# GpSimd's subtractions issued in pieces of at most 256 columns, in a kernel of one transform and two networks

## The chip, the core and the metric

The kernel runs on one core of a Trainium2 chip. A core has five engines that run their own instruction streams and wait for one another by semaphores: TensorE (PE in the profile, its weight loads PEld), VectorE (DVE), ScalarE (ACT), GpSimd (POOL) and SyncE (SP), which here issues the DMAs. The metric is the device time of one execution in microseconds; less is better.

## The reference

```python
def _attn_ref(x):                      # x: (2, 3008, 256)
    X = np.fft.fft(x, axis=1)
    X = np.fft.fft(X, axis=2)
    return X.real.astype(np.float32)

def _moe_ref(x, w_in, w_out):          # 6016 tokens, 256 -> 2048 -> 256
    h = x @ w_in
    r = np.maximum(h, 0.0)
    g = r * r
    return (g @ w_out).astype(np.float32)

def _moe2_ref(x, w_in, w_out):         # the same sizes
    h = x @ w_in
    g = h * (1.0 / (1.0 + np.exp(-1.702 * h)))
    return (g @ w_out).astype(np.float32)
```

The real part of a two-dimensional Fourier transform feeds a first network with a squared ReLU, whose output feeds a second network with a sigmoid gate. All of it is in single precision (the weights arrive as float64 and are narrowed on the chip).

## The kernel before

**Numbers as two parts.** The kernel's matmuls take operands of type `fp32r`, to which a cast loses bits of the float32. So each operand `x` is kept as a high part, a cast of `x` by ScalarE, and a low part `x - high`, a subtraction. A product is three matmuls: high x high, high x low and low x high. The low parts are all made by one helper:

```python
def sub(eng, o, a, b):
    eng.tensor_tensor(out=o, in0=a, in1=f32(b), op=ALU.subtract)
```

`eng` is VectorE (`V`) or GpSimd (`G`). As the helper is one line, every such subtraction has line L75 in the profile, on either engine; they are told apart by the tile that they write.

**Who calls it.** `low_part` (L700) makes `gl`, the low part of a hidden activation: two rows of 376 or 378 columns, on GpSimd in 113 of 128 steps and on VectorE in the steps of `VSTEPS`. `split_eo` (L335) makes the low part of `eo`, the transformed input. `widen` (L175) does it for a weight tile `w` of 1024 columns, on the engine that the table `LOW` names. `widen_in` (L209) prepares the second network's first weights: four sums on GpSimd (L221), then for each of two rows a pair of subtractions into `w2i`, of 512 columns (four groups of 128) and 384 columns (three groups of 128). `split` and the second network's `gl` (L830) use VectorE alone.

**First stage (to about 528 us).** A loop of 128 steps works through the first network. The tokens are 8 blocks (2 batches x 4 groups of frequencies) of 376 or 378 columns times two rows; a step is one block and one of 16 groups of 128 hidden features. In a step:

- `front1` issues six matmuls (L429 to L431) into one of two `psa` buffers in PSUM
- VectorE makes `p` (L686) and the two halves of `h` (L688, L689) out of that buffer, which frees it
- ScalarE takes the ReLU (L695) and the square (L696), and casts the high part `gh` (L698); in the steps of `SV` VectorE does ReLU and square in one (L693)
- `low_part` of the step before is issued: `gl = h - gh`. Tiles of `h` have four buffers, those of `gh` and `gl` five each
- `back` issues the 12 matmuls (L444) of the step four earlier (`LAG`), from its `gh` and `gl`
- `background(i)` adds items of other work, by the table `PLAN` (first step, items a step, last step). From step 18 on, background work of VectorE and ScalarE is queued behind the step's own.

Background work is the folds and the transform of the inputs (L260 to L278, L293, L332), and the preparation of weights: `narrow` turns the two 32-bit words of a float64 into a float32 in about six operations of 1024 columns (L157 to L168, most on VectorE), then `widen` or `widen_in` casts and subtracts. Near the end, the first block of the second network's input is added up and differenced on GpSimd (L581, L591).

In this stage the order of instructions on each engine is set by a planner: it takes ready instructions by priority (their order in the code) on times that it models, so an engine's order can differ from the code's.

**Second stage (from about 528 us).** The second network, 64 units of two hidden groups in a seven-product scheme (L737) with its second matmuls (L753), is written in the order of issue by hand (`manual_schedule`). Its low parts are VectorE's; GpSimd has only L581 and L591.

Of the kernel before, what the change touches and what calls it, by code (L numbers as in the profile page):

```python
# [13 lines left out]
ALU = mybir.AluOpType  # L14
# [48 lines left out]
def spectral_two_mlps_kernel(  # L63
# [5 lines left out]
    V, A, G, T = nc.vector, nc.scalar, nc.gpsimd, nc.tensor  # L69

    def f32(ap):
        return ap.bitcast(F32)

    def sub(eng, o, a, b):
        eng.tensor_tensor(out=o, in0=a, in1=f32(b), op=ALU.subtract)  # L75


    psa = ctx.enter_context(tc.tile_pool(name="psa", bufs=2, space=PSUM))
# [96 lines left out]
    def widen(mlp, kind, g, temps, dest, then=None, tag="xt"):  # L175
        low = G if LOW[mlp, kind, g] == "G" else V
        raw = raws.pop((mlp, kind, g))
        ue = temp(temps, tag)
        yield from narrow(raw, ue, (mlp, kind, g))
        if then:  # L180
            then()
        w = dest.tile([P, 2, 1024], F32R, tag="w", name="w")
        o = ue[:, 0]
        if (mlp, kind) == (0, 0):

            o = ue[:, 1]
            a, c = ue[:, 0, 0:512], ue[:, 0, 512:1024]
            yield lambda: (G if g in EOG else V).tensor_tensor(out=o[:, 0:512], in0=a, in1=c, op=ALU.add)
            yield lambda: V.scalar_tensor_tensor(out=o[:, 512:1024], in0=a, scalar=mask, in1=c,
                                                 op0=ALU.mult, op1=ALU.subtract)  # L190
        yield lambda: A.copy(w[:, 0], o)
        yield lambda: sub(low, w[:, 1], o, w[:, 0])
        if mlp and (kind, g) in PARKED:
            park((mlp, kind, g), w)
        weights[mlp, kind, g] = w
# [13 lines left out]
    def widen_in(g, ue, dest, then=None):  # L209

        raw = raws.pop((1, 0, g))
        yield from narrow(raw, ue, (1, 0, g))
        if then:
            then()
        a = ue[:, 0].rearrange("p (k r f c) -> p k r f c", k=2, r=2, f=2)
        t = ue[:, 1].rearrange("p (i r c) -> p i r c", i=4, r=2)
        a11, a21, a12, a22 = (a[:, k, :, f] for k in range(2) for f in range(2))
        s2, s3, s4 = (t[:, i] for i in range(3))
        for o, x, y, op in ((s3, a11, a21, ALU.subtract), (a21, a21, a22, ALU.add), (s2, a21, a11, ALU.subtract),
                            (s4, a12, s2, ALU.subtract)):  # L220
            yield lambda: G.tensor_tensor(out=o, in0=x, in1=y, op=op)  # L221
        for r in range(2):
            w = dest.tile([P, 2, 1024], F32R, tag="w", name="w2i")
            parts = []
            for lo, hi, x in ((0, 4, a[:, :, r]), (4, 7, t[:, 0:3, r])):
                o = w[:, :, lo * P:hi * P]
                o = o.rearrange("p h (k f c) -> p h k f c", k=2, f=2) if lo == 0 else o.rearrange("p h (i c) -> p h i c", c=P)
                parts.append((o[:, 0], o[:, 1], x))
            yield lambda: [A.copy(o, x) for o, _, x in parts]
            yield lambda: [sub(G, l, x, o) for o, l, x in parts]  # L230
            if (0, g) in PARKED:
                park((1, 0, 2 * g + r), w)
            weights[1, 0, 2 * g + r] = w
# [101 lines left out]
    def split_eo(b, kb, e):  # L335
        wd = WID[kb]
        low = V if LOWE[b, kb] == "V" else G
        t = ep.tile([P, 2, 2, NP], F32R, tag="eo", name="eo")
        for r in (slice(0, 1), slice(1, 2)) if (b, kb) in FINE else (slice(0, 2),):
            A.copy(t[:, r, 0, 0:wd], e[:, r, 0:wd])  # L340
            sub(low, t[:, r, 1, 0:wd], e[:, r, 0:wd], t[:, r, 0, 0:wd])
        eo[b, kb] = t
# [317 lines left out]
    for i in range(n):  # L660
# [19 lines left out]
        elif done:  # L680
# [6 lines left out]
                               in1=ps[:, 0, 0:wd], op0=ALU.mult, op1=ALU.add)  # L687
# [74 lines left out]
    with tc.manual_schedule():  # L762
        for u in range(units + 2):
# [41 lines left out]
            if here:  # L805
                if p == 7 and j < BLKS - 1:
                    run(stage_a(j + 1))
                if rest is not None and not run(rest, 3 if j else (0, 2, 2, 4, 4, 4, 4, 4)[p]):
# [8 lines left out]
                                in1=cd[:, :, 0:wd], op=ALU.add)  # L817
# [20 lines left out]
        o = m3.tile([P, 2, NP], F32, tag="o", name="o")  # L838
# [133 lines left out]
```

## Time and profile before

| what | us |
|---|---|
| median of 3 runs | 1037.11 (1035.15 to 1038.47) |
| profiled execution, its own time | 1035.54 |
| span of its instructions | 1033.8 |
| TensorE busy | 971.6 |
| VectorE busy | 817.1 |
| ScalarE busy | 616.4 |
| GpSimd busy | 351.4, in 216 instructions |

The profile is one execution. The span runs from the first instruction to the last; the rest of the execution's time lies around it. Busy times are sums over the whole span, and the two stages differ: the share of an engine in one of them is read from a view by stretch. A duration of VectorE or GpSimd runs from the start of an instruction to its end, with whatever held it up once it had started; a wait for another engine's result lies ahead of the start and is shown as idle time with the releaser.

### The profile page before, as it was taken

To read this page: it belongs to the slowest core of one execution; us is meant where nothing else is said; L and a number is where in the kernel's file an instruction comes from. 1 tells how busy PE (TensorE), PEld (TensorE's weight loads), DVE (VectorE), ACT (ScalarE), POOL (GpSimd) and SP (SyncE) were. 2 spreads that over 40 slices of the span, in tenths; PEclk is the share of its full clock that TensorE was granted. 3 is DMA by queue.
4 is the path that set the end of the run, shared out by engine and by line. 5 is a ranking of instruction groups with operands and counts; after the bars stand their busy time and mean duration, and the time that the engine had idled before them with its cause. 6 is when DMAs were issued, how large, how long until landed. Compare 5 with 4: busy or idle time off the path is not lost.

```text
span 1033.8 us, 14043 instructions
## 1 busy us (share of the span) xinstructions
PE 971.6 (94%) x5496; PEld 939.3 (91%) x5496; DVE 817.1 (79%) x1088; ACT 616.4 (60%) x764; POOL 351.4 (34%) x216
## 2 busy tenths in 40 slices
PE   4879997899989999999989999999999999999998
PEld 4569887899989889898989999999999999999997
DVE  7995889886777579777658888887988888888875
ACT  2667576775788578797754554554555445454443
POOL 2546464444567446786815210102020020200000
PEclk9999999999999999999999999999999999999999
DMA  7531112101132112101342101000100001000000
GB/s 289 204 127 61 71 71 82 71 31 53 42 129 96 72 55 99 71 31 60 120 132 93 60 31 31 30 31 5 57 1 31 30 26 35 1 31 1 30 1 30
DMA packets 22914, 65.22 MB, mean 63 GB/s; under 512 B 1856, under 2 KB 14272, under 8 KB 19648
## 3 DMA queue, kind: packets, MB, share of 16 engines
q1 hardware_dynamic: 22848, 64.32, 17.4%
q8 instruction: 43, 0.70, 0.3%
q14 instruction: 23, 0.19, 0.1%
HBM read 43.13 MB, written 21.19 MB: 62 GB/s over the span
## 4 chain that ended last, share of the span: by engine, by line
PE 47%; DVE 5%; ACT 4%; issue 1%; POOL 1%; DMA 0%; DVEq 0%; POOLq 0%; ACTq 0%
PE psb L753 24%; PE psa L737 22%; ACT h L696 1%; ACT h L695 1%; DVE gl L75 1%; PE psb L444 1%; ACT gh L698 1%; POOL gl L75 1%; DVE g L789 0%; DVE ue L168 0%; DVE h L689 0%; DMA ydram<-o 0%; DVE p L686 0%; POOL raw L581 0%; DVE h L688 0%
## 5 line engine op out<-in xcount | busy, mean ns | idle before, releaser
L75 POOL TENSOR_TENSOR gl<-h,gh 128x752 fp32r<-128x752 f32 (+1 forms) x113 | 216.0, 1920 | 166.6 <-ACT gh L698 142.1
L444 PE MATMUL psb<-gh,w 128*128 128x376 f32 (+1 forms) x1024 | 240.6, 340 | 4.4 <-ACT o L557 3.5
L753 PE MATMUL psb<-gh,w 128*128 128x376 f32 (+1 forms) x1024 | 237.7, 334 | 0.0
L444 PEld LDWEIGHTS psb<-gh,w 128*128 128x128 f32 x1024 | 185.6, 192 | 6.8 <-ACT o L557 4.7
L753 PEld LDWEIGHTS psb<-gh,w 128*128 128x128 f32 x1024 | 182.9, 188 | 0.0
L695 ACT ACTIVATE h<-h 128x752 f32<-128x752 f32 (+1 forms) x116 | 96.5, 833 | 81.7 <-DVE h L689 77.8
L444 PE MATMUL psb<-gl,w 128*128 128x376 f32 (+1 forms) x512 | 133.7, 341 | 3.2 <-POOL gl L75 2.8
L818 ACT ACTIVATE g<-c 128x1128 f32<-128x1128 f32 (+1 forms) x64 | 73.7, 1152 | 100.1 <-DVE c L816 100.1
L753 PE MATMUL psb<-gl,w 128*128 128x376 f32 (+1 forms) x512 | 129.9, 335 | 0.4 <-DVE gl L75 0.3
L686 DVE SCALAR_TENSOR_TENSOR p<-n,w1n_t,psa 128x376 f32<-128x376 f32 (+1 forms) x128 | 76.5, 601 | 59.7 <-PE psa L431 59.5
L698 ACT CAST gh<-h 128x752 fp32r<-128x752 f32 (+1 forms) x128 | 105.0, 822 | 21.5 <-DVE h L693 14.0
L75 DVE TENSOR_TENSOR gl<-g,gh 128x1504 fp32r<-128x1504 f32 (+1 forms) x64 | 112.2, 1753 | 1.6 <-ACT gh L798 1.6
L429 PE MATMUL psa<-eo,w 128*128 128x376 f32 (+1 forms) x256 | 89.9, 351 | 24.6 <-DVE h L689 19.9
L798 ACT CAST gh<-g 128x1504 fp32r<-128x1504 f32 (+1 forms) x64 | 93.1, 1454 | 32.2 <-DVE g L789 32.2
L591 POOL TENSOR_TENSOR ue<-raw 128x376 f32<-128x376 f32 (+1 forms) x16 | 19.6, 1243 | 271.0 <-DVE ya L75 270.8
L444 PEld LDWEIGHTS psb<-gl,w 128*128 128x128 f32 x512 | 94.6, 193 | 4.8 <-POOL gl L75 4.0
L696 ACT ACTIVATE h<-h 128x752 f32<-128x752 f32 (+1 forms) x116 | 96.6, 834 | 3.2
L753 PEld LDWEIGHTS psb<-gl,w 128*128 128x128 f32 x512 | 92.2, 188 | 1.0 <-DVE gl L75 1.0
L789 DVE TENSOR_TENSOR g<-g,c 128x1128 f32<-128x1128 f32 (+1 forms) x64 | 89.6, 1401 | 1.2 <-ACT g L818 1.2
L815 DVE TENSOR_TENSOR g<-g,psa 128x376 f32<-128x376 f32 (+1 forms) x64 | 35.0, 547 | 68.5 <-ACT g L814 68.5
L430 PE MATMUL psa<-eo,w 128*128 128x376 f32 (+1 forms) x256 | 86.4, 338 | 0.7 <-DVE eo L75 0.7
L431 PE MATMUL psa<-eo,w 128*128 128x376 f32 (+1 forms) x256 | 86.2, 337 | 0.0
(135 smaller groups left out, 1594.3 us busy)
## 6 DMA issues: line engine op xcount, KB each, us to landing
ydram<-o SPq DMA_DIRECT2D x18, 376.0 KB, 2.9
xt<-in_x SPq DMA_DIRECT2D x5, 1024.0 KB, 7.1
cst<-in_dfts SPq DMA_DIRECT2D x8, 570.0 KB, 5.5
raw<-ydram SPq DMA_DIRECT2D x6, 752.0 KB, 4.5
out<-o SPq DMA_DIRECT2D x11, 376.0 KB, 3.1
raw<-in_w1i SPq DMA_DIRECT2D x4, 1024.0 KB, 5.6
raw<-in_w1o SPq DMA_DIRECT2D x4, 1024.0 KB, 4.9
raw<-in_w2i SPq DMA_DIRECT2D x4, 1024.0 KB, 4.9
```

Of the source, the lines that this page charges most:

```text
L75: eng.tensor_tensor(out=o, in0=a, in1=f32(b), op=ALU.subtract)
L429: T.matmul(o, lhsT=w[:, 0, fs], rhs=t[:, par, 0, 0:wd], start=True, stop=False)
L430: T.matmul(o, lhsT=w[:, 0, fs], rhs=t[:, par, 1, 0:wd], start=False, stop=False)
L431: T.matmul(o, lhsT=w[:, 1, fs], rhs=t[:, par, 0, 0:wd], start=False, stop=True)
L444: T.matmul(acc[j][ec][:, s, 0:wd], lhsT=w[:, hl, e0:e0 + P], rhs=(gh, gl)[gi][:, s, 0:wd], start=(first and hl == 0 and gi == 0), stop=(la ...
L695: A.activation(out=hv, in_=hv, func=AF.Relu)
L696: A.activation(out=hv, in_=hv, func=AF.Square)
L698: last_a = A.copy(gh[:, :, 0:wd], hv)
L737: T.matmul(bank, lhsT=w[:, hl, slot * P:(slot + 1) * P], rhs=t[:, yl, i], start=(first and hl == 0 and yl == 0), stop=(hl == 1), skip_grou ...
L753: T.matmul(o[:, s, 0:wd], lhsT=w[:, hl, e0:e0 + P], rhs=g[:, 2 * i + s, 0:wd], start=(f == 0 and hl == 0 and g is gh), stop=(f == 15 and h ...
L789: V.tensor_tensor(out=g[:, 1:4, 0:pw], in0=g[:, 1:4, 0:pw], in1=c[:, :, 0:pw], op=ALU.mult)
L798: A.copy(gh[:, :, 0:pw], g[:, :, 0:pw])
```

## The change

The helper splits what it issues to GpSimd. A tile with more than two dimensions is taken apart along its second one until pieces are rows; a row of `w` columns is cut into `ceil(w / 256)` nearly equal parts. VectorE's subtractions stay whole, and so do GpSimd's other operations (L188, L221, L260, L581, L591), which don't go through the helper.

```diff
+    def pieces(*aps):
+
+        if len(aps[0].shape) > 2:
+            for i in range(aps[0].shape[1]):
+                yield from pieces(*(ap[:, i] for ap in aps))
+        else:
+            w = aps[0].shape[1]
+            k = -(-w // 256)
+            for i in range(k):
+                yield tuple(ap[:, i * w // k:(i + 1) * w // k] for ap in aps)
+
     def sub(eng, o, a, b):
-        eng.tensor_tensor(out=o, in0=a, in1=f32(b), op=ALU.subtract)
+        for o, a, b in pieces(o, a, b) if eng is G else ((o, a, b),):
+            eng.tensor_tensor(out=o, in0=a, in1=f32(b), op=ALU.subtract)
```

So two rows of 376 columns become four instructions of 188 columns, two rows of 378 four of 189, 1024 columns four of 256, and a `w2i` pair seven of 128.

## Rows read from the trace of the kernel before

**Rows 1.** The page, part 1: busy us of each engine (share of the span), instructions.

```profile
PE 971.6 (94%) x5496; PEld 939.3 (91%) x5496; DVE 817.1 (79%) x1088; ACT 616.4 (60%) x764; POOL 351.4 (34%) x216
```

**Rows 2.** Busy time by stretch; columns: length, PE, PEld, DVE, ACT, POOL, clock, DMA.

```profile
14.00:528.00 514.00, 468.34 (x2595) 439.26 (x2594) 398.40 (x588) 363.33 (x464) 294.56 (x179) 0.98 0.25 89
480.00:528.00 48.00, 43.11 (x240) 41.96 (x239) 28.12 (x45) 35.65 (x46) 32.71 (x19) 0.96 0.42 148
528.00:1033.80 505.80, 500.70 (x2894) 497.48 (x2892) 411.32 (x488) 251.75 (x299) 53.07 (x31) 1.00 0.09 30
```

**Rows 3.** TensorE's waits, 14 to 528 us: us in total, times, longest.

```profile
PE psa L429 <- DVE h L689: 19.9, 15, 3.2
...
PE psb L444 <- ACT o L557: 3.5, 2, 2.0
...
PE psb L444 <- POOL gl L75: 2.8, 3, 1.5
```

**Rows 4.** VectorE's groups by shape, 14 to 528 us: busy, mean ns, idle before.

```profile
L166 DVE SCALAR_TENSOR_TENSOR ue<-raw,ue 128x1024 uint32<-128x1024 uint32 x16 | 25.6, 1601 | 1.5 <-ACT ue L163 1.4
L168 DVE CUSTOM_DVE_ANT_0 ue<-ue 128x2048 uint16<-128x2048 uint16 x16 | 24.0, 1498 | 0.1
L158 DVE TENSOR_SCALAR ue<-ue 128x1024 f32<-128x1024 f32 x16 | 20.4, 1277 | 6.8 <-ACT ue L157 6.8
...
L165 DVE TENSOR_SCALAR ue<-raw 128x1024 uint32<-128x1024 uint32 x8 | 13.3, 1658 | 3.0 <-POOL w2i L75 3.0
```

**Rows 5.** The timeline, VectorE around 40 and 521 us: start, duration, instruction.

```profile
36.68 0.69 DVE L158 TENSOR_SCALAR ue<-ue 128x1024 f32<-128x1024 f32 x1
...
43.29 2.29 DVE L158 TENSOR_SCALAR ue<-ue 128x1024 f32<-128x1024 f32 x1
45.50 1.21 DVE L168 CUSTOM_DVE_ANT_0 ue<-ue 128x2048 uint16<-128x2048 uint16 x1
...
521.17 1.96 DVE L75 TENSOR_TENSOR yc<-raw,yc 128x756 fp32r<-128x756 f32 x1 [4.24 <-ACT yc L598]
```

**Rows 6.** The timeline, 463 to 474 us; in brackets idle time before it.

```profile
464.41 4.08 POOL L75 TENSOR_TENSOR gl<-h,gh 128x752 fp32r<-128x752 f32 x2
464.50 2.30 DVE L165 TENSOR_SCALAR ue<-raw 128x1024 uint32<-128x1024 uint32 x1 [0.48 <-POOL w2i L75]
...
466.71 2.33 DVE L158 TENSOR_SCALAR ue<-ue 128x1024 f32<-128x1024 f32 x1
...
469.48 1.81 DVE L159 TENSOR_SCALAR ue<-ue 128x1024 uint32<-128x1024 uint32 x1
...
472.12 1.21 DVE L166 SCALAR_TENSOR_TENSOR ue<-raw,ue 128x1024 uint32<-128x1024 uint32 x1
472.25 0.44 PE L429 MATMUL psa<-eo,w 128*128 128x376 f32 x1 [1.79 <-DVE h L689]
```

**Rows 7.** GpSimd's groups by line, whole span: busy, mean ns, idle before.

```profile
L75 POOL TENSOR_TENSOR gl<-h,gh 128x752 fp32r<-128x752 f32 (+1 forms) x113 | 216.0, 1920 | 166.6 <-ACT gh L698 142.1 <-issue 8.3 <-DVE h L693 6.9
...
L75 POOL TENSOR_TENSOR w<-ue,w 128x1024 fp32r<-128x1024 f32 x8 | 19.6, 2454 | 15.3 <-ACT w L191 15.3
...
L75 POOL TENSOR_TENSOR w2i<-ue,w2i 128x512 fp32r<-128x512 f32 (+1 forms) x16 | 18.7, 1194 | 2.0 <-ACT w2i L229 2.0
...
L221 POOL TENSOR_TENSOR ue<-ue 128x256 f32<-128x256 f32 x16 | 11.9, 742 | 3.3 <-DVE ue L168 2.5
```

**Rows 8.** The timeline, 488 to 507 us: GpSimd's run and who waits for it.

```profile
488.12 3.48 POOL L581 TENSOR_TENSOR raw<-raw,ue 128x1512 f32<-128x1512 f32 x1
...
493.35 1.82 POOL L591 TENSOR_TENSOR ue<-raw 128x378 f32<-128x378 f32 x2
...
497.03 9.21 POOL L75 TENSOR_TENSOR gl<-h,gh 128x752 fp32r<-128x752 f32 x5
...
498.86 0.55 DVE L688 TENSOR_TENSOR h<-p,psa 128x376 f32<-128x376 f32 x1 [0.73 <-POOL gl L75]
498.88 0.61 PE L444 MATMUL psb<-gl,w 128*128 128x376 f32 x2 [1.05 <-POOL gl L75]
```

## The prediction, made blind

> **What bounds the kernel now.** Read the engine totals first: TensorE is busy 971.6 us of the span of 1033.8, VectorE 817.1, GpSimd 351.4 [rows 1]. GpSimd looks harmless there, so the second view is the table by stretch, cut where the first network ends and the second begins [rows 2]. From 528 us on TensorE is busy 500.7 of 505.8 us: matmuls alone set the time, and the subtractions of that stage are VectorE's. From 14 to 528 us it is busy 468.3 of 514.0: 45.7 us of idle time, and GpSimd is busy 294.6 us. Everything that this change can give is in those 45.7 us.
>
> Third, who TensorE waits for in that stretch [rows 3]. The largest entry is the first-layer matmul (L429) waiting for VectorE's `h` (L689), 19.9 us in 15 waits: the two PSUM buffers of `front1` are still unread, so VectorE is late. Waits for GpSimd's `gl` are 2.8 us.
>
> Fourth, why VectorE is late: its own groups in that stretch [rows 4]. The preparation of weights has fixed shapes, so each group should have one duration. It hasn't. L158 means 1277 ns, L165 1658, L166 1601, L168 1498. Undisturbed, L158 took 0.69 us, L168 1.21 [rows 5], and L166 1.21 [rows 6]; L165 is of L158's kind and width, so I take 0.69. The excess is 16 x 0.59 + 8 x 0.97 + 16 x 0.39 + 16 x 0.29 = 9.4 + 7.8 + 6.2 + 4.6 = 28.0 us. Read one by one in the same way (duration less the shortest of its shape), VectorE has 51 such delays over 0.1 us, the first and the last of more than a microsecond at 43.29 and 521.17 us [rows 5], and they sum to 55.5 us. The first is 2.29 - 0.69 = 1.60; the last is a subtraction of 756 columns that shows 1.96.
>
> Fifth, what holds them: the timeline around 465 us [rows 6]. GpSimd starts two `gl` at 464.41, 4.08 us together. L165 starts 0.09 us later and shows 2.30, so its own 0.69 begins about when the first `gl` is over. L158 starts at 466.71, inside the second `gl`, shows 2.33, and ends half a microsecond after that one does. L159 meets the third. The pattern is a resource held for a whole instruction: VectorE's delay is what is left of GpSimd's instruction, and VectorE gets in at its end, even with the next `gl` queued (the pair took 4.08 us where two alone take 3.7). L688, which reads one operand from PSUM, doesn't suffer: 0.55 us at 498.86, inside a run of five `gl` [rows 8]. The three delays make `h` late, and TensorE stands 1.79 us before L429 at 472.25. Of the 55.5 us, 49 have a `sub` of L75 as the holder and 6 the folds and sums that the change leaves alone (L260, L188).
>
> **The change, part by part.**
>
> *Instructions.* A `gl` or `eo` of two rows of 376 becomes four pieces of 188; a weight of 1024 columns four of 256; a `w2i` pair (512 + 384) four and three of 128. So 113 + 3 + 8 + 16 = 140 instructions of GpSimd [rows 7] (the three `eo` are not in those rows) become 452 + 12 + 32 + 56 = 552. Only the first of a tile has to wait for its inputs.
>
> *Price of a piece.* No 188-column subtraction is in the trace. With no fixed cost, half of a 378-column one, of which two take 1.82 us [rows 8], gives 0.45 us. From above stands the 256-column group, L221, at 0.742 [rows 7]; scaled to 188 at 2.2 ns a column (1024 against 256 columns: 2454 - 742 over 768) it gives 0.59. L221's four depend on one another and are strided, so I take the middle, 0.53. Then a `gl` costs 2.12 against 1.84 alone (9.21 / 5, [rows 8]): +0.28, x113 = 32 us. A weight is 4 x 0.68 = 2.7 against 2.45: +2 us over eight. A `w2i` pair is 7 x 0.40 = 2.8 against 2 x 1.19 = 2.4: +3 over eight. With `eo`, about +38 us: GpSimd 294.6 -> 333 of 514. Lying beside other work this costs nothing on average: GpSimd's idle time covers it and `gl` is used four steps after `h`. It shows where GpSimd is already behind, from 488 to 506 us: L581, four of L591 and five `gl` in a row, with VectorE (0.73) and TensorE (1.05) waiting for `gl` [rows 8]. There the extra is 6 x 0.28 = 1.7 us; for the first weights, `eo` and the other waits for `gl` I add 2.3. Cost on the path: +4 us.
>
> The Trainium skill ("GPSIMD Engine Reference", section 3.1) lists 4497 ns for a two-input addition of 2048 columns; with this trace's 2.45 for 1024 that leaves a fixed 0.4 us an instruction, and by it a piece would be an estimated 0.78. The trace's 0.91 for 378 columns speaks against that: such a fixed part would leave 1.3 ns a column. By the page the change would cost more than it gives (third rival).
>
> *Delays of VectorE.* A delay is bounded by the piece instead of the whole: at most about 0.53 - 0.13 = 0.40 us (0.13 is how much sooner VectorE's work starts than the holder's recorded end), 0.2 in the middle. GpSimd then takes its next piece, so the next operation in VectorE's run meets one too, and the stretched `gl` meets more of them. I count 70 meetings at 0.2 = 14 us in place of 49; bounds are 46 x 0.1 = 5 us, and 35 if every operation meets a full piece. So 14 to 44 us of VectorE's time come back; I take 35.
>
> *What of this reaches TensorE.* Not all: in stretches where TensorE is full, a delay is hidden. The part that surfaces stands in TensorE's 19.9 us before L429 [rows 3]. Delays fall by 35 of 55.5, 63%, and 63% of 19.9 is 12.5 us. (From 14 us of VectorE's time it would be 5, from 44 it would be 15.8.) What is late next at 472 us is ScalarE's ReLU and square behind `h`; they have the four steps' slack.
>
> *Sum.* -12.5 + 4 = -8.5 us. The profiled execution took 1035.5 (span 1033.8 and 1.7 around it), so 1027.0. The median of the runs, 1037.1, is 1.6 above that execution; I keep 1027, because smaller items of VectorE before TensorE, left out of the sum, point the same way.
>
> *What the row can't show.* The first stage is laid out by a planner that orders ready instructions by modelled times; 412 more instructions on GpSimd can swap work on every engine. No row prices it; I leave +-6 us.
>
> **The rivals.**
>
> 1. *Hidden anyway* (same). VectorE's delays fall, but TensorE's idle time moves to ScalarE's `o` (3.5 us [rows 3]) and GpSimd, and the new order takes the rest. For it: only 45.7 us are idle at all. Against it: 15 of the waits are on `h`. A gain of 4 and the cost of 4: 1035.5 us.
>
> 2. *No hand-over between pieces.* If GpSimd's queued next piece keeps the resource, VectorE waits for the whole run as now and GpSimd's 38 us come on top, of which the same 4 surface: 1035.5 + 4 = 1039.5. Against it: L165 got in between two queued `gl` [rows 6].
>
> 3. *GpSimd becomes the bound* (slower). Place: 420 to 510 us, where it works through `gl`, weights and sums back to back. At 0.742 a piece, a `gl` is 2.97, +1.13 on 1.84. From 480 to 528 us GpSimd is busy 32.7 of 48 [rows 2], and each of the 13 `gl` there adds 1.13, 14.7 in all: full. Six lie in the back-to-back run, +6.8; `h` buffers, freed by the last piece, come late and VectorE stands, so about 13 us over the stage with the run before it, against 7 that remain of the gain: 1035.5 + 13 - 7 = 1041.5. It decides from about 0.65 us a piece, where the extra (0.76 x 113 = 86 us) uses most of the idle time left to GpSimd in its crowded stretches. For it: L221's row; against it: the 378s.
>
> 4. *More comes back.* L689's whole 19.9 us and the 2.8 before `gl` vanish, and the granted clock, 0.98 in this stretch against 1.00 after [rows 2], recovers with them: 22 us go, 1013.5.
>
> **How the numbers follow.** Forecast (1018 to 1033) 0.57; rival 4 0.07; rival 1 0.13; rival 2 0.07; rival 3 0.16. Within 0.3% of 1037.1, which is what a measurement of this kernel can tell from no change, is 1034 to 1040. Faster: 0.57 + 0.07 = 0.64. Same: rival 1 and a little of rival 2, 0.15. Slower: 0.21. The range must reach rival 3 to leave out no more than 2 in 10, and below to rival 4: 1013 to 1042.
>
> **What would show it.** L158, L165 and L159 at means under 0.95 us, L166 and L168 under 1.4: the delay step. Pieces at 0.45 to 0.6 us and GpSimd at about 390 us over the span: the price. TensorE's wait for L689 down to some 8 us: the path step. From 528 us on the same 505 us. I am wrong if pieces are over 0.65, if L158 stays above 1.1, or if the order on VectorE or TensorE is visibly another and TensorE waits more for `gl`.

## The result: slower by 0.65%

The changed kernel takes 1044.36 us (median of ten runs, 1039.15 to 1047.02), the kernel before 1036.52 on the same chip (also ten, one of them an outlier of 5342.97 us). The two medians are 0.76% apart; the ratio on record, without the outlier, is 1.0065 [1.0052, 1.0077]: slower, where 1027.0 was forecast. The profiled execution is the quickest of the ten, 1039.15 us, so the trace below explains less than the median shows; a second profiled run at 1046.11 us (experiment 2) supplies the rest.

Engine totals of the changed kernel, from its page: busy us, share of the span, instructions.

```profile
span 1037.4 us, 14453 instructions
PE 972.1 (94%) x5496; PEld 942.1 (91%) x5496; DVE 799.2 (77%) x1088; ACT 616.9 (59%) x764; POOL 448.7 (43%) x628
```

Its groups answer [rows 7]: busy, mean ns, idle before.

```profile
L87 POOL TENSOR_TENSOR gl<-h,gh 128x188 fp32r<-128x188 f32 (+1 forms) x452 | 299.4, 698 | 92.3 <-ACT gh L710 73.0 <-issue 10.1 <-POOL gl L87 4.0
...
L87 POOL TENSOR_TENSOR w<-ue,w 128x256 fp32r<-128x256 f32 x32 | 25.5, 828 | 11.0 <-ACT w L203 11.0
L87 POOL TENSOR_TENSOR w2i<-ue,w2i 128x128 fp32r<-128x128 f32 x56 | 25.2, 488 | 0.0
```

GpSimd has the 412 instructions more that were counted, but 97 us more work where 38 were forecast [rows 1]. VectorE has 18 us less. The order of instructions on TensorE, VectorE, ScalarE and SyncE is the same in both kernels, so the term of +-6 us for reordering is nothing.

The table by stretch of the changed kernel, against [rows 2]: stretch, length, then busy us and count of PE, PEld, DVE, ACT, POOL, then granted clock, DMA share, GB/s.

```profile
14.00:528.00 514.00, 467.25 (x2586) 440.75 (x2584) 377.82 (x584) 362.05 (x462) 391.02 (x590) 0.97 0.24 87
420.00:480.00 60.00, 48.19 (x260) 46.48 (x261) 41.73 (x56) 42.16 (x53) 51.22 (x86) 0.93 0.13 44
...
528.00:1037.40 509.40, 502.93 (x2904) 499.45 (x2904) 414.49 (x493) 253.60 (x301) 54.00 (x33) 1.00 0.09 32
```

In this trace the loss is in one stretch, 420 to 480 us: TensorE is busy 48.2 of 60 us there, and GpSimd 51.2. The same stretch of the kernel before:

```profile
420.00:480.00 60.00, 53.98 (x297) 51.97 (x296) 48.33 (x67) 48.84 (x62) 42.05 (x28) 0.97 0.12 44
```

TensorE's waits, 14 to 528 us, answer [rows 3]; below them two of VectorE's own.

```profile
PE psa L441 <- DVE h L701: 15.2, 9, 5.7
PE psb L456 <- POOL gl L87: 9.5, 12, 1.8
PE psb L456 <- ACT o L569: 7.0, 2, 6.4
```

```profile
DVE ue L177 <- POOL w2i L87: 11.4, 2, 6.8
DVE h L700 <- POOL gl L87: 5.8, 8, 1.3
```

Without its longest, 5.7 us, the wait for `h` is 9.5 us in eight places, half of what it was: that part of the forecast did happen. Two long waits, and more and longer ones for `gl` (2.8 before), took its place. VectorE's groups answer [rows 4]: busy, mean ns, idle before.

```profile
L178 DVE SCALAR_TENSOR_TENSOR ue<-raw,ue 128x1024 uint32<-128x1024 uint32 x16 | 22.5, 1408 | 1.5 <-ACT ue L175 1.4
L180 DVE CUSTOM_DVE_ANT_0 ue<-ue 128x2048 uint16<-128x2048 uint16 x16 | 21.8, 1363 | 0.1
L170 DVE TENSOR_SCALAR ue<-ue 128x1024 f32<-128x1024 f32 x16 | 13.4, 838 | 10.7 <-ACT ue L169 10.7
L177 DVE TENSOR_SCALAR ue<-raw 128x1024 uint32<-128x1024 uint32 x8 | 14.9, 1865 | 11.4 <-POOL w2i L87 11.4
```

Three of the four fell about as forecast. L177 (L165 before) rose, and it also started late: 11.4 us of idle time behind `w2i`, 3.0 before. The timeline around the two places shows both; start, duration, in brackets the idle time before. "Held out" is used below for a VectorE operation that has started and has to let several of GpSimd's instructions pass.

```profile
418.65 2.91 POOL L87 TENSOR_TENSOR w2i<-ue,w2i 128x128 fp32r<-128x128 f32 x7
421.60 2.68 DVE L177 TENSOR_SCALAR ue<-raw 128x1024 uint32<-128x1024 uint32 x1 [6.83 <-POOL w2i L87]
421.60 1.13 ACT L169 ACTIVATE ue<-raw 128x1024 f32<-128x1024 f32 x1 [7.28 <-POOL w2i L87]
422.62 0.78 ACT L569 COPY o<-psb 128x752 f32<-128x752 f32 x1
423.45 0.99 PE L456 MATMUL psb<-gh,w 128*128 128x376 f32 x2 [6.36 <-ACT o L569]
...
466.56 2.98 POOL L87 TENSOR_TENSOR w2i<-ue,w2i 128x128 fp32r<-128x128 f32 x7
469.48 6.59 POOL L87 TENSOR_TENSOR gl<-h,gh 128x188 fp32r<-128x188 f32 x12
469.58 7.05 DVE L177 TENSOR_SCALAR ue<-raw 128x1024 uint32<-128x1024 uint32 x1 [4.58 <-POOL w2i L87]
479.31 0.68 PE L441 MATMUL psa<-eo,w 128*128 128x376 f32 x1 [5.71 <-DVE h L701]
```

At the first place it is not L177 that TensorE waits for. ScalarE's L169 (L157 before) needs the same `w2i`: it stands 7.28 us here and 2.07 in the kernel before. The copy `o` (L569) is next on ScalarE and releases TensorE at 423.45 us, before L177 has ended. TensorE waits 6.36 us here and 2.02 before. So this loss comes from GpSimd's run and not from the hold-out: that run ends at 421.6 us, 0.3 us later than before, and whatever was ahead by then waits for it.

Read the last four lines, the second place, against [rows 6]: the same operation at the same step got in there at the end of the first `gl`, with another queued. Here twelve pieces, three whole `gl`, pass while it stands. The `h` behind it comes late, and TensorE stands 5.71 us where it stood 1.79.

Both long waits have a second cost, TensorE's clock. In this trace the granted clock falls while TensorE stands idle in each of them, and it stays at its lower level, 0.50 or 1.2 GHz, for 3.6 and 5.7 us after TensorE has started again (columns as above):

```profile
420.20:427.00 6.80, 3.55 (x11) 3.55 (x12) 5.40 (x6) 4.19 (x5) 4.60 (x10) 0.50 0.29 107
478.20:485.00 6.80, 5.69 (x18) 5.69 (x19) 6.59 (x11) 5.32 (x7) 0.26 (x1) 0.50 0.00 0
```

In the kernel before only 473.3 to 476.7 us is at that level between 411 and 500 us. Matched matmul by matmul (as in the table below), TensorE restarts at 423.45 us 0.3 us behind the kernel before and is 1.6 behind at 428: the lower clock goes with 1.3 of the first loss. No run holds the clock fixed, so that share is read off and not tested.

**Where the time goes, by pairing.** The 5496 matmuls run in the same order in all these kernels, so the start of the same one can be subtracted between two traces. Each row is one execution. This is its lag against the kernel before (us; negative is ahead), at times of the kernel before. The rows from the third on are the experiments below:

```
                     75     174    411    424    464    473    500    530
change, 1039.15     +2.1   -5.3   -4.0   +0.9   +1.0   +7.4   +6.9   +3.7
change, 1046.11     +1.7   -5.6   -3.9   +1.0   +1.2   +7.7   +8.4  +10.6
gl, eo cut          +0.6   -7.8   -8.3   -4.9   -5.1   -0.1   +1.6   +2.4
w2i cut             +0.8   +1.1   +3.4   +4.8   +4.8   +6.9   +7.3   +7.1
w cut               +2.6   +1.7   +2.1   +2.1   +2.6   +2.5   +2.7   +3.7
gl in four, 16-94   +2.3   -4.7   -5.0   -3.4   -3.3   -3.1   -3.0   -2.4
gl in two           +0.9   -6.6   -9.6   -8.9  -10.2   -7.9   -8.9  -10.3
two, 64 columns     +1.0   -6.5   -9.1   -8.4   -8.1  -10.1   -9.8  -12.8
four, longer op     +1.4   -7.0   -8.2   -4.0   -0.4   -0.8   +0.3   -1.4
```

Up to 411 us the change is 4 us ahead. At the two places, 421 and 470 us, it loses 11.

### The profile page after: what moved, and what is told of

Its sections match the earlier page's. It is cut to its first block, busy times and chain, and to the rows that moved or that the text cites. A ratio compares the mean times of both kernels' runs of the same rounds, so it can differ in the third digit from the quotient of the medians.

```text
span 1037.4 us, 14453 instructions
## 1 busy us (share of the span) xinstructions
PE 972.1 (94%) x5496; PEld 942.1 (91%) x5496; DVE 799.2 (77%) x1088; ACT 616.9 (59%) x764; POOL 448.7 (43%) x628
## 4 chain that ended last, share of the span: by engine, by line
PE 51%; DVE 3%; POOL 2%; ACT 1%; issue 1%; DVEq 0%; POOLq 0%; ACTq 0%
PE psb L765 24%; PE psa L749 22%; PE psb L456 3%; POOL gl L87 1%; DVE ue L177 1%; DVE gl L87 1%; POOL w2i L87 1%; PE psa L441 0%; PE psa L443 0%; PE psa L442 0%; DVE g L801 0%; POOL ue L233 0%; ACT h L707 0%; ACT h L708 0%; ACT gh L710 0%
## 5 line engine op out<-in xcount | busy, mean ns | idle before, releaser
L87 POOL TENSOR_TENSOR gl<-h,gh 128x188 fp32r<-128x188 f32 (+1 forms) x452 | 299.4, 698 | 92.3 <-ACT gh L710 73.0
L456 PE MATMUL psb<-gl,w 128*128 128x376 f32 (+1 forms) x512 | 136.4, 343 | 9.5 <-POOL gl L87 9.5
L765 PE MATMUL psb<-gl,w 128*128 128x376 f32 (+1 forms) x512 | 129.9, 335 | 0.4 <-DVE gl L87 0.3
```

The costliest lines, as they stand in the source:

```text
L456: T.matmul(acc[j][ec][:, s, 0:wd], lhsT=w[:, hl, e0:e0 + P], rhs=(gh, gl)[gi][:, s, 0:wd], start=(first and hl == 0 and gi == 0), stop=(la ...
L765: T.matmul(o[:, s, 0:wd], lhsT=w[:, hl, e0:e0 + P], rhs=g[:, 2 * i + s, 0:wd], start=(f == 0 and hl == 0 and g is gh), stop=(f == 15 and h ...
```

## The experiments

Theory at first: a VectorE operation that meets pieces is sometimes held out over many, and that costs the time. Rivals: the pieces themselves cost it, on GpSimd's path; or the weights do.

**1. Widths and short runs by themselves.** A kernel of nothing but GpSimd runs and single VectorE operations:

```
for k in range(count):      # GpSimd, each to its own columns
    run[k] = a[0:width] - b[0:width]
u = f(raw)                  # VectorE, released just before the run
```

> Computes nothing of the reference; it measures two costs by themselves. First GpSimd alone, subtractions of 64 to 1024 columns back to back: with a fixed part f and 2.2 ns a column, theory 'price' (GpSimd's longer total is what costs) expects f near 0.14 us, so 0.55 for 188 columns; were the changed kernel's mean of 0.66 the undisturbed price, f would be 0.25. Then 32 trials: VectorE's one operation is released by a GpSimd instruction behind which a run of 12 x 188, 6 x 376 or 3 x 752 columns is queued; VectorE has been idle 0 to 8 us before it. Theory 'held out' expects the one-input operations (L170's and L177's forms) to wait for the end of the whole run of 12, some 6 us, when VectorE was idle for over 4 us, and less than 0.6 us when another VectorE operation runs just before; the two-input forms wait 0.4 us in every trial. Rival: all forms wait 0.4 us in all trials, and the 6.36 us in the changed kernel have another cause.

VectorE always got in after the first instruction of the run, whatever its form and however long it had been idle (6 to 13 us): a one-input form took 1.05 us behind 188 columns, against 0.68 undisturbed. So it isn't a matter of the operation's form after an idle time, and the theory of this expectation missed. What held L177 out doesn't show in runs met at their first piece.

**2. The change once more.**

> The changed kernel once more. Its ten runs fall into two heaps, 1039.2 to 1040.5 and 1043.6 to 1047.0, and the profile in hand is the fastest of all. 'Held out' expects a run of the slower heap to have one or two more VectorE operations of 2 us or more (weight preparation, L170 or L177), at other places than 421.6 and 469.6 us, and the lag behind the kernel before to jump there by 3 to 6 us. 'Price' expects the same durations of GpSimd everywhere and the difference spread out.

1046.11 us. The two hold-outs come again (421.65, 2.68 us; 469.82, 7.05 us), and one more stands where the quicker execution had none. The same operation in the quicker one took 0.75 us:

```profile
513.33 3.31 DVE L87 TENSOR_TENSOR yb<-raw,yb 128x378 fp32r<-128x378 f32 x1
```

Six pieces pass, and its excess is 2.6 us; by 530 us this run is 6.9 us behind the quicker one (table). But the lag does not jump where the operation stands, as the expectation had it. TensorE is 3.1 us behind the quicker run when this operation starts, and no more until 530 us. A `gl` came 1.5 us later at 506 us, and the granted clock was at its lower level from 508.6 to 512.0 us, which goes with 1.5 more. As far as the trace tells, the hold-out reaches TensorE only at 533.90 us, through VectorE's later work: a wait of 3.39 us for `u` where the quicker run waited 1.64 (1.8 more lag). The lower clock around that wait, 532.5 to 539.3 us, goes with the last 1.9. So about half of what separates the two executions goes with the clock, and under 2 us with the extra hold-out.

**3. L177 as a two-input operation** for three of its groups.

```diff
-V.tensor_scalar(out=eu, in0=lw, scalar1=2.0 ** -29, scalar2=None, op0=ALU.mult)
+V.scalar_tensor_tensor(out=eu, in0=lw, scalar=2.0 ** -29, in1=lw, op0=ALU.mult, op1=ALU.min)
```

> The changed kernel with one difference: in three of the second network's weight groups L177 is written as an operation with two inputs (the same input twice, with a minimum that changes nothing), 1.21 us in place of 0.69 undisturbed. 'Held out' expects the 7.05 and 2.68 us of L177 to become about 1.6, TensorE's waits of 5.7 us at 479 us to shrink to under 2, and the time to fall from 1044 to 1036 to 1039. 'Price' expects no gain: 1044, or 1 us more for the longer operation, since GpSimd stays late by the same.

1046.69 us, 1.010 [1.008, 1.012]. A miss: the operations held out belong to other groups than the three that I changed. But a two-input operation was held out in this run too (`yb` at 510.79 us, 6.83 long), so that form doesn't escape, and TensorE waited 2.43 us for the `h` behind it.

**4. Which subtractions cost.** Parts of the change alone; the subtractions named in each expectation as whole are called with `False`.

```diff
-def sub(eng, o, a, b):
-    for o, a, b in pieces(o, a, b) if eng is G else ((o, a, b),):
+def sub(eng, o, a, b, cut=True):
+    for o, a, b in pieces(o, a, b) if eng is G and cut else ((o, a, b),):
...
+        yield lambda: sub(low, w[:, 1], o, w[:, 0], False)
...
+            yield lambda: [sub(G, l, x, o, False) for o, l, x in parts]
```

> Only gl and eo are cut into pieces; the weights w and w2i stay whole (so L177's release by w2i comes some 0.7 us sooner for each pair). 'Held out' expects the runs of gl pieces behind w2i to be there still, so one or two waits of L177 over 2 us remain and the time is 1041 to 1045. 'Price' by the weights' share expects about a tenth of the extra to go (7 of 90 us of GpSimd's time), and most of the loss, which sits behind w2i: 1036 to 1040.

> Only the subtractions of the weights (w, w2i) are issued in pieces; gl and eo stay whole. The kernel with gl and eo alone cut took 1038.2 us and the full change 1044.4, so the weights' pieces cost about 6 us there. If that is the pieces' own price: 1041 to 1043 us here. If it comes only from longer runs of pieces in front of gl's pieces, 1036 to 1038, no difference from the kernel before, and no VectorE operation delayed by more than 2 us.

> Only w's subtractions (8 of 1024 columns, in four pieces each) are cut; w2i, eo and gl whole. The weights together cost 6.8 us (1043.8 against 1037.1). GpSimd has 0.87 us more per w, 7 us in all, and 5.6 us more in w2i. If the price is GpSimd's own time on the path, both share it: 1040 to 1041 us. If it is w2i alone, which stands before the held-out operations at 421 and 472 us: 1036 to 1038. If w alone: 1042 to 1044.

> Only w2i's subtractions are cut (56 pieces of 128 columns in place of 16 instructions); gl, w and eo whole. w and w2i cut took 1043.8 us, w alone 1037.7, before 1036.9. Each of the four groups of w2i takes GpSimd about 1.3 us longer, and the same TensorE instructions fell behind by 1.35, 1.40, 2.10 and 1.03 us at four places between 300 and 505 us. If these are all on the path: 1042 to 1044 us. Rival, w2i costs only behind a late w: 1038 to 1040.

```
gl and eo cut   1038.24   1.0008 [0.9996, 1.0021]
w and w2i cut   1043.82   1.0062 [1.0045, 1.0080]
w cut           1037.71   1.0011 [1.0002, 1.0020]
w2i cut         1041.94   1.0052 [1.0038, 1.0066]
```

The parts add up to the whole (1.0008 + 1.0062 against 1.0065). Of the weights' 0.62%, 0.52 is `w2i`'s, 5.4 us: 56 pieces of 128 columns in place of 16 instructions. Here is its trace, VectorE's wait and the two places:

```profile
DVE ue L177 <- POOL w2i L87: 5.8, 2, 3.9
```

```profile
426.08 2.26 DVE L177 TENSOR_SCALAR ue<-raw 128x1024 uint32<-128x1024 uint32 x1 [3.92 <-POOL w2i L87]
470.75 4.09 DVE L177 TENSOR_SCALAR ue<-raw 128x1024 uint32<-128x1024 uint32 x1 [1.90 <-POOL w2i L87]
```

With only `w2i` cut, L177's wait grows by 2.8 us; with only `gl` cut by 5.6 (8.6); with both by 8.4 (11.4). GpSimd's run in front of the two places, from the end of its last sum (L221 before) to L177's start, grew by 2.8, 3.7 and 6.6 us: `w2i`'s extra time goes one to one into VectorE's wait, and with `gl` cut some 1.8 us of it are not GpSimd's longer run. At 470.75 the operation is held out over two *whole* `gl`, so pieces of `gl` aren't needed for that; in experiment 6, with nothing cut in this stretch, it was so again (461.21 us, 4.09 us).

The same two places with only `gl` and `eo` cut:

```profile
415.89 2.68 DVE L177 TENSOR_SCALAR ue<-raw 128x1024 uint32<-128x1024 uint32 x1 [5.44 <-POOL w2i L87]
417.73 0.83 PE L456 MATMUL psb<-gh,w 128*128 128x376 f32 x2 [4.93 <-ACT o L569]
462.02 7.07 DVE L177 TENSOR_SCALAR ue<-raw 128x1024 uint32<-128x1024 uint32 x1 [3.12 <-POOL w2i L87]
471.78 0.68 PE L441 MATMUL psa<-eo,w 128*128 128x376 f32 x1 [5.73 <-DVE h L701]
```

Here `gl` in pieces gives 8.3 us up to 411, loses 3.4 at the first place, where the hold is hardly longer than before (2.68 against 2.25) but the idle time in front of it is 2.9 us longer, and TensorE again waits for ScalarE's `o`; and it loses 5.0 at the second.

**5. When VectorE is held out.** Long runs by themselves: the same, but the `m`-th of the run writes `u`, so that it releases VectorE.

> A measurement of GpSimd and VectorE by themselves; it computes nothing of the reference. GpSimd runs through m equal subtractions without a wait, the m-th of them releases one VectorE operation (a one-input operation of 1024 strided columns, 0.68 us by itself; in four trials a two-input one of 752 columns), and 5 to 16 further subtractions follow. Widths 64, 188, 376 and 752. Theory A, the number of instructions already run through decides: at 188 columns VectorE gets in after one piece up to m = 10 (1.0 to 1.1 us) and is held out over five or more pieces from m = 14 or 16 on (4 us and more); at 64 columns, where twenty pieces take only 7.7 us, it is held out at m = 20 as well; at 752 it gets in after one instruction up to m = 8 although 14 us have gone by, and is held out at m = 16. Theory B, the time since VectorE last got in decides (about 7 us): at 752 columns it is held out from m = 4 on, at 64 columns not at m = 12. Theory C, neither does: nothing is held out here for more than two pieces, and what held it out in the kernel (up to 7.05 us) lies outside GpSimd's run.

> A second measurement of GpSimd and VectorE by themselves; it computes nothing of the reference. The first one let VectorE in after one instruction when it was released by the 14th of a run at 188 columns or the 12th at 752, and kept it out to the run's end from the 16th on. Here: where between them the limit lies; whether a hold-out of 40 pieces ends before the run does; and what sets the count back. If the count is of instructions since GpSimd last had to share, then a VectorE operation let in at the 8th makes the 20th (12 later) short, 1.05 us, and the 28th (20 later) held out, 9 us; the same for a pause of GpSimd of some 0.5 us after the 8th if a pause sets it back. If the count runs over the whole run regardless, both are held out. If one entry or pause frees the rest of the run, both are short.

In the first run, the first two lines are 188 columns, released by the 14th and the 16th of the run; then 752 columns, by the 12th and the 16th.

```profile
92.48 1.05 DVE L60 TENSOR_SCALAR Uw188m14x<-raw 128x1024 uint32<-128x1024 uint32 x1 [15.98 <-POOL Uw188m14x L44]
110.60 9.15 DVE L60 TENSOR_SCALAR Uw188m16x<-raw 128x1024 uint32<-128x1024 uint32 x1 [17.06 <-POOL Uw188m16x L44]
...
262.80 2.24 DVE L60 TENSOR_SCALAR Uw752m12x<-raw 128x1024 uint32<-128x1024 uint32 x1 [27.92 <-POOL Uw752m12x L44]
299.86 9.14 DVE L60 TENSOR_SCALAR Uw752m16x<-raw 128x1024 uint32<-128x1024 uint32 x1 [34.82 <-POOL Uw752m16x L44]
```

At these widths the number of instructions decides, not the time: twelve of 752 columns are 21 us and let VectorE in, sixteen of 188 are 8.6 us and don't. The limit is soft: in the second run the 14th of 188 columns already shut VectorE out, the 14th of 752 did not and the 15th did. Once out, it stays out to the end of the run (64 columns differ, see the last section). From that second run, forty pieces behind the 17th; then a run in which VectorE got in at the 8th (line 1 of the pair), released again by the 20th; then the same with a VectorE operation at the 8th that reads one operand from PSUM; then with GpSimd made to wait once after the 8th:

```profile
174.33 22.03 DVE L69 TENSOR_SCALAR Uw188m17a40x<-raw 128x1024 uint32<-128x1024 uint32 x1 [9.63 <-POOL Uw188m17a40x L44]
...
221.51 1.06 DVE L66 TENSOR_SCALAR Earlyentryx<-a 128x1024 f32<-128x1024 f32 x1 [4.79 <-POOL Earlyentryx L44]
228.41 1.05 DVE L69 TENSOR_SCALAR Uw188m20a16entryx<-raw 128x1024 uint32<-128x1024 uint32 x1 [5.85 <-POOL Uw188m20a16entryx L44]
...
273.74 9.12 DVE L69 TENSOR_SCALAR Uw188m20a16twox<-raw 128x1024 uint32<-128x1024 uint32 x1 [5.91 <-POOL Uw188m20a16twox L44]
...
319.26 1.05 DVE L69 TENSOR_SCALAR Uw188m20a16waitx<-raw 128x1024 uint32<-128x1024 uint32 x1 [11.74 <-POOL Uw188m20a16waitx L44]
```

Here an entry or a pause sets the count back; the PSUM operation (0.55 us, as undisturbed) does not. With 28 in place of 20 all three are held out, 20 instructions after the entry or pause.

These runs also give the price of a piece without neighbours: one every 0.278 us at 64 columns, 0.540 at 188, 0.933 at 376, 1.725 at 752, that is 0.144 us + 2.10 ns a column. For 188 columns the forecast's 0.53 stands by itself, and rival 3's 0.742 doesn't. The prediction's estimate of 0.78 from the figure of the Trainium skill ("GPSIMD Engine Reference", section 3.1) is refuted too.

**6. Other sizes and places.** The limit at 512 columns; and, with `w` and `w2i` whole, `gl` in four pieces in steps 16 to 94 only, `gl` in two everywhere, `gl` in two up to step 94.

```diff
-            k = -(-w // 256)
+            k = -(-w // 512)
...
-            sub(G if i not in VSTEPS else V, gl..., h..., gh...)
+            sub(G if i not in VSTEPS else V, gl..., h..., gh..., 16 <= i < 95)
```

> The same change with 512 columns as the limit: gl is two pieces of 376 columns. By the slope measured for single widths (1.04 us at 376 where the same columns are written again, 0.79 at 256) a gl takes some 1.9 to 2.0 us, against 1.78 whole and 2.20 in four. If the number of instructions in an undisturbed run decides when VectorE is held out, runs are half as long in number, nothing is held out over more than two pieces outside the weights, and the time is 1029 to 1033 us. If time decides, the hold-outs at 421 and 469 us stay (2.7 and 7 us), and the time is 1037 to 1042.

> gl is issued in pieces in steps 16 to 94 only (from about 107 to 403 us), whole before and after, w and w2i whole. In the kernel with all of gl cut the same TensorE instructions ran 2 us late at 49 us, 7.7 us early from 173 to 365 us, and lost all of it between 411 and 499 us behind two held-out VectorE operations. Theory, the gain of the middle is real and is lost to the hold-outs alone: the 8 us stay and the time is 1027 to 1031 us. Rival, the gain is slack that the crowded stretch takes back whatever is cut there (GpSimd or the weights end last): 1034 to 1038 us with the early lead gone by 500 us.

> gl in two pieces of 376 columns in all steps, w and w2i whole. The limit of 512 with the weights cut gave 1031.1 us, 5.9 less than before; gl in four with the weights whole 1038.2. If the weights' pieces cost by themselves, as 1043.8 us for the weights alone says, this is 4 to 6 us less than the limit of 512: 1025 to 1028 us. Rival, at 512 the weights' pieces are fewer (w two, w2i still of 128 columns) and cost little: 1030 to 1032.

> As the kernel with gl in two, but gl whole from step 95 on (about 400 us), where VectorE was held out behind runs of pieces. If the pieces cost there more than they give (2.2 us lost at 416 us and 3.3 at 468 in the kernel with the limit of 512): 2 to 4 us below the kernel with gl in two. Rival, whole gl's keep VectorE out over two instructions as well (4.1 us at 461 us in the kernel with only the middle steps cut) and nothing is won: within 1.5 us of it.

```
limit 512, all               1031.13   0.9939 [0.9919, 0.9958]
gl in four, steps 16 to 94   1031.20   0.9941 [0.9922, 0.9960]
gl in two, weights whole     1028.33   0.9913 [0.9899, 0.9928]
the same up to step 94       1029.97   0.9934 [0.9922, 0.9945]
```

All four beat the kernel before. Against `gl` in four everywhere, cutting only the middle brings 7 us (0.9941 and 1.0008). Between 411 and 530 us it loses 2.6 of its lead and the other 10.7 (table): in that stretch four pieces cost 8 us more than whole ones. Two pieces don't: whole ones there gain nothing (the rival of the last expectation). That with 512 nothing is held out over more than two pieces was wrong, though. One stayed (459 us, 6.25 us), and with `gl` in two as well (455 us, 6.32 us). From start to start a whole `gl` takes 1.78 us, two pieces 1.92 in this kernel's runs, four 2.20; with two GpSimd comes nearly as early as before, and a delay of VectorE that ends with one piece is about half as long; for the hold-out that is not so.

**7. Breaking the runs in the kernel.** In steps 95 to 112 VectorE gets one more operation after `h`, on the dead tile `p`; first 64 columns, then all of them with two inputs. `w` and `w2i` are whole. The planner also moved some other operations of VectorE and ScalarE in that stretch, so these runs differ from their partners by more than the added operation.

```diff
+        if 95 <= i < 113:
+            V.tensor_scalar(out=p[:, 0:64], in0=p[:, 0:64], scalar1=0.5, scalar2=2.0, op0=ALU.max, op1=ALU.min)
...
+            V.tensor_tensor(out=p[:, 0:wd], in0=p[:, 0:wd], in1=p[:, 0:wd], op=ALU.subtract)
```

> gl and eo in four pieces, w and w2i whole, and in steps 95 to 112 VectorE, after each step's h, also runs one added operation on 64 columns of the dead tile p (its result is used by nothing). By itself GpSimd's run was set back when VectorE was let in: with that, no run reaches 13 pieces here, and the operations held out at 416 and 462 us for 2.7 and 7.05 us come in after one piece (under 1.2 us). The time goes from 1038.2 us to 1030 to 1034: about 6 of the 9 us lost between 411 and 499 us come back, less some 18 added operations in VectorE's idle time. Rival, the hold-out there has another cause, or 64 columns do not set the run back: 1037 to 1040 us with the operation at 462 us still held out over 6 us.

> gl in two pieces, w and w2i whole, with the same added operation in steps 95 to 112. The kernel with gl in two took 1028.3 us and held VectorE out for 5.6 us at 455 us, over six pieces; it lost 2 us of its lead there. Theory: 1025 to 1027 us, nothing held out for over 1.5 us. Rival: 1028 to 1030.

> As the kernel with gl in four and an added VectorE operation in steps 95 to 112, but the added operation is a two-input one over 376 columns of the dead tile p, some 0.45 us, where 64 columns took under 0.2 and left GpSimd's pieces at their usual 0.55 us a piece, so that the operation at 462 us was held out for 7.1 us all the same. If what sets the run back is a pause that GpSimd really makes, this one makes it: the operation at 462 us comes in under 1.5 us, and the time is 1030 to 1034 us. Rival, an entry in the kernel does not set the run back at all: held out over 6 us again, 1037 to 1041 us.

> gl in two, w and w2i whole, with the added operation of 376 columns. With 64 columns the operation at 455 us came in after one piece (1.48 us, 6.3 us without it) and the kernel took 1025.9 us. Theory: the operation comes in under 1.5 us again; VectorE has some 18 times 0.3 us more to do, in idle time for the most part: 1025 to 1028 us. Rival, the added time is on the path: 1029 to 1032.

```
gl in four, 64 columns   1037.05   1.0012 [0.9995, 1.0029]
gl in two, 64 columns    1025.91   0.9901 [0.9882, 0.9920]
gl in four, longer       1038.47   1.0017 [1.0001, 1.0032]
gl in two, longer        1032.73   0.9962 [0.9950, 0.9974]
```

The second place in the first three of them:

```profile
462.03 7.10 DVE L177 TENSOR_SCALAR ue<-raw 128x1024 uint32<-128x1024 uint32 x1 [2.69 <-POOL w2i L87]
```

```profile
456.68 1.48 DVE L177 TENSOR_SCALAR ue<-raw 128x1024 uint32<-128x1024 uint32 x1 [0.70 <-POOL w2i L87]
```

```profile
465.98 1.07 DVE L177 TENSOR_SCALAR ue<-raw 128x1024 uint32<-128x1024 uint32 x1 [2.37 <-POOL w2i L87]
```

With `gl` in four, 64 columns fitted in between pieces without GpSimd pausing. At the second place the hold-out stayed; at the first one L177 came in after one piece (1.06 us, 2.68 without). With `gl` in two it came in at the second place after 1.48 us where it had been held out for 6.32, though GpSimd's twelve instructions in front of it show no pause in either run. So a short entry helped in two places and not in a third, and no count of instructions read here tells them apart: the theory as I had put it missed.

With the longer operation GpSimd did pause, and L177 came in after one piece at both places, with `gl` in four and in two. So in the kernel, too, the hold-out ends where GpSimd's run is broken by pauses. But the time did not come back. With `gl` in four, the pauses made GpSimd 3.3 us later between the two places (from L177's one start to the other, 49.4 us against 46.1), and TensorE lost 3.6 us between 424 and 464 us (last line of the table), nearly as much as the end of the hold-out gave. With `gl` in two the longer operation cost more than it gave, near the last expectation's rival. There the short operation had turned 2.3 us lost at 464 to 473 into 2.0 won; its median is the best of all, but its interval overlaps that of `gl` in two alone.

At the first place the hold-out itself cost TensorE nothing: with it gone (64 columns, `gl` in four), TensorE still waited 4.97 us for ScalarE's `o`, 4.93 with it.

## Why the prediction was wrong, step by step

- *Instructions.* Right: 412 more.
- *Price of a piece.* Right by itself (0.53 forecast, 0.540 measured; `w2i` 0.42 against 0.40). GpSimd's growth was forecast at 38 us and is 97. `gl` went from 216.0 to 299.4 us [rows 7]. About 47 of these 83 are the pieces (2.20 - 1.78, x113). The other 36 are GpSimd's own delays behind VectorE: 75 pieces are longer than the rest, each with a VectorE operation beside it, by 46.7 us in all, where 25 whole `gl` were, by 11.2. That price of the hand-over the sum left out.
- *Delays of VectorE.* Forecast 55.5 to 20.5 us, measured 35 in some 60 delays. Most are below 0.46 us, as the hand-over said. The 11 longer ones sum to 16.7 us: 8.4 are the two hold-outs of L177 (6.4 in one), 5.0 stand behind folds that the change leaves whole. The sentence "GpSimd then takes its next piece" held for short runs only. Rival 2 described these two operations, and was wrong elsewhere.
- *What reaches TensorE.* Its sign held up to 411 us: -4.0 us with all cut, -8.3 without the weights' pieces, against -12.5 + 4. So some 8 of the 12.5 us came.
- *Cost on the path, +4 us.* **This is the step that failed.** I priced it from 488 to 506 us and spread the rest over GpSimd's idle time. But L165 at 421 and 464 us already waited for `w2i` (3.0 us in [rows 4], 0.48 in [rows 6]), and so did ScalarE's L157 (2.07 at 421 us). There GpSimd runs without a pause, and what is added to its run is added to their start. `w2i`'s pieces cost 5.4 us there and around it (forecast: +3 of GpSimd's time, held to lie beside other work), `w`'s about 1, and `gl`'s pieces in that stretch about 8 (experiment 6): some 14 us in place of 4. At the first place this is late start alone; at the second it is late start and hold-out together, and their shares were not separated. TensorE's lower clock behind the long waits is in these sums; the prediction had it only in rival 4, as a gain.
- *Rivals.* The third had the place (420 to 510 us) and the end (1041.5) nearly right, and the extra too: it took 86 us for `gl`, measured are 83. Its price of a piece was wrong by itself (0.540, not 0.65 or more), but in the kernel, delays behind VectorE included, a piece took 299.4 / 452 = 0.66 us. So two signs of being wrong that the prediction named did show: pieces over 0.65, and TensorE waiting more for `gl` (9.5 us, 2.8 before). The point at which GpSimd becomes the bound was worked out from its idle time over the stage, and not from the run in front of L165, where there was none.

The Trainium skill ("SBUF — State Buffer", on SBUF's two separate sides) calls the port pair that VectorE and GpSimd share an exclusive lock for a whole instruction, with the other one blocked until then. The short runs agree (1.05, 1.45 and 2.24 us behind 188, 376 and 752 columns). After some 14 to 16 instructions of 188 to 752 columns without a pause the measurements differ: the block lasts to the end of the run, 22.03 us in the longest.

## What to carry to other kernels

A helper engine at a third of its time can be the bound of a stretch: look for the operations, on any engine, that already wait for it, and add the whole extra of the run in front of them to the path. Cutting an instruction for another engine's sake pays until the fixed part (0.144 us here) makes the run longer than the shorter waits are worth: two pieces gave -0.87%, four +0.08%, and 128-column pieces alone +0.52%. And in these runs smaller pieces did not let VectorE in once GpSimd had run long enough without a pause.

## Not expected of the hardware

In runs by themselves, at 188 to 752 columns, VectorE's entry is decided by the number of GpSimd instructions since the last entry or pause (some 14 to 16), not by their width or time, and hardly by VectorE's form. In the kernel the limit is less sharp: with nothing cut from step 95 on, L177 was held out over two whole `gl` at 461.21 us, behind some eight instructions after the last pause in its trace, and let in after one at the same step of the kernel before. At 64 columns it was let in again near the 26th of a run wherever it had been released from the 18th to the 24th (2.83, 1.72, 1.17 us); why, no run shows. What in the chip keeps the count was not tried.
